# A side bank opened to VectorE's scores, history copies moved to GpSimd and the plan replaced, in a fused attention kernel with a tuned schedule

## The chip, the cores and the metric

The kernel runs on one core of a Trainium2 chip. The metric is the device time of one execution in microseconds (us); spans from the trace are about 2 us shorter than the time of the same execution. Each run also reports the mean granted clock of TensorE, 1.000 being full speed. A ratio of two kernels is the mean time of one kernel's fast runs over the mean of the other's fast runs of the same rounds, so it isn't quite the ratio of the medians that are quoted. The experiments ran on several chips, each beside runs of the kernel before; where two of them ran on different chips, the ratios are the fairer comparison.

## The reference, cut to what matters

```python
# x: 2048 tokens x 640, bf16; two branches of 32 heads of 20
A: scores = q @ k.T / sqrt(20); p = softmax(scores); o_A = (p @ v) @ woA      # all 2048 keys
B: keys at distance 0, 2, 4 .. 14 only; softmax over the 8; o_B = (...) @ woB
g = sigmoid(x . gate_w);   out = g * o_A + (1 - g) * o_B
```

Branch A is nearly all of the work: 32 groups (8 sets of four heads by 4 query blocks) of 64 units. A **unit** is 128 keys by 512 queries of one head, so there are 2048 units, and each needs an exponential of 128 x 512.

## The kernel before

A unit's exponential is made by ScalarE or by VectorE. ScalarE takes two or three units in one instruction, a **visit**. VectorE adds a constant and reads the bits as a number (`uD`), and for accuracy makes three shifted copies (`eD`) of every four such units, a **quad**; each copy costs TensorE one more round of products with the values. The program uses eight banks of PSUM, the memory that TensorE writes: two score buffers of three banks, an output bank, and a side bank for everything else (projections, branch B, the output product), called side work here.

```python
BANKS = [(sbank, 0), (score[0], 1024), (score[1], 1024)]   # side bank; third bank of each score buffer

# side work asks for a bank: the side bank wins when both are free
for b in range(NB):
    if not bank_used[b] and b != xheld[0] and (best is None or
            max(bank_free[b], now) < max(bank_free[best], now)):
        best = b
...
# next_tile: three units if the third bank of this buffer is free, else two;
# a unit for VectorE ("ride") can only have that same third bank
free = not bank_used[x] and bank_free[x] <= now + XTOL and not crowded(x)
n = 3 if free else 2
...
    if len(us) == 2 and not ride:
        ride = wanted([...])          # is VectorE early enough, is a quad open or may one be opened?
        if ride: break
```

The program orders its instructions while it is built. It keeps an assumed clock for each engine, and at each visit decides from these clocks what goes next: side work, fillers (matmuls with a zero operand or into a free bank, which keep TensorE busy), VectorE's units. Some eighteen thresholds steer it, and `PLAN` can change them at every tenth visit. The end of its assumed clocks is called the **scheduler's estimate** below. It is no measurement.

Of the kernel before, what the change touches and what calls it, by code (L numbers as in the profile page):

```python
# [9 lines left out]
I16 = mybir.dt.int16  # L10
ALU = mybir.AluOpType
# [39 lines left out]
    0: ((0.34, 0.64), 0.37, 6.3, 2.5, 0.51, -1.0, -0.1, 11.8, 4.5, 7.2, 0.52, 0.47, 4.4, 1.86, 0.0, 0.85, 2, 0.0),  # L51
    10: ((0.34, 0.64), 0.37, 6.3, 2.5, -0.17, -1.0, -0.1, 13.02, 4.5, 7.2, 0.52, 0.47, 4.4, 1.86, 0.0, 0.85, 2, 0.0),
    20: ((0.34, 0.64), 0.21, 6.3, 6.6, -0.17, -1.0, -0.1, 13.02, 4.5, 8.28, 0.52, 0.47, 4.4, 1.86, 0.0, 0.85, 2, 0.0),
    30: ((0.28, 0.52), 0.35, 2.5, 6.6, 0.49, -1.55, -0.55, 9.24, 6.7, 7.2, 0.53, 0.57, 4.23, 4.64, 0.02, 0.85, 2, 1),
    50: ((0.28, 0.52), 0.35, 2.5, 6.6, 0.49, -1.55, -0.55, 9.24, 6.7, 7.2, 0.25, 0.57, 4.23, 4.64, -0.13, 0.85, 2, 1),
    60: ((0.28, 0.52), 0.35, 2.5, 6.6, 0.49, -1.55, -0.55, 9.24, 6.7, 7.2, 0.53, 0.57, 4.23, 4.28, 0.16, 0.85, 2, 1),
    70: ((0.28, 0.52), 0.1, 2.5, 6.6, 0.49, 0.2, -0.55, 9.24, 6.7, 7.2, 0.5, 0.57, 4.23, 4.64, 0.02, 0.85, 2, 1),
    80: ((0.28, 0.52), 0.34, 2.5, 5.5, 0.49, -1.55, -0.62, 9.24, 7.0, 7.2, 0.53, 0.57, 4.55, 4.64, 0.02, 0.85, 2, 1),
    90: ((0.28, 0.52), 0.3, 2.5, 6.6, 0.49, -1.55, -0.55, 9.24, 6.7, 7.8, 0.5, 0.57, 4.23, 4.64, 0.02, 0.85, 2, 1),
    110: ((0.28, 0.52), 0.3, 2.5, 6.6, 0.49, -1.55, -0.55, 8.84, 6.7, 7.8, 0.5, 0.57, 4.23, 4.64, 0.02, 0.85, 2, 0),  # L60
    120: ((0.28, 0.52), 0.3, 5.5, 6.6, 0.49, -1.34, -0.55, 8.84, 6.7, 7.8, 0.5, 0.57, 4.23, 4.64, 0.05, 0.85, 2, 0),
    130: ((0.28, 0.52), 0.19, 5.5, 6.3, 0.49, -0.24, -0.53, 9.24, 6.7, 11.3, 0.53, 0.57, 4.23, 4.93, -0.13, 0.89, 2, -3),
    140: ((0.28, 0.52), 0.3, 2.5, 2.5, 0.87, -1.55, -0.55, 8.84, 6.7, 7.8, 0.5, 0.57, 3.8, 4.64, 0.02, 0.85, 2, 0),
    170: ((0.28, 0.52), 0.3, 2.5, 2.5, 0.87, -1.28, -0.55, 8.42, 6.7, 7.8, 0.5, 0.54, 3.8, 4.64, 0.02, 0.85, 2, 0),
    180: ((0.28, 0.52), 0.39, 6.6, 2.5, 0.87, -1.55, -0.65, 10.03, 6.7, 7.8, 0.5, 0.57, 3.8, 3.83, 0.02, 0.87, 2, -3),
    190: ((0.28, 0.52), 0.19, 2.5, 2.5, 0.7, -1.55, -0.55, 7.32, 6.7, 7.8, 0.5, 0.5, 3.8, 2.96, 0.02, 0.85, 2, -3),
    200: ((0.23, 0.54), 0.35, 2.5, 2.5, 0.87, -1.55, -0.55, 7.13, 6.7, 7.71, 0.5, 0.57, 3.46, 4.13, 0.02, 0.86, 2, -3),
    210: ((0.28, 0.52), 0.3, 2.5, 2.5, 0.9, -1.55, -0.6, 7.13, 6.7, 7.71, 0.5, 0.49, 3.46, 4.64, 0.02, 0.85, 2, -3),
    220: ((0.32, 0.54), 0.3, 2.5, 2.5, 1.16, -1.55, -0.6, 7.13, 6.7, 7.71, 0.5, 0.49, 3.46, 4.64, 0.02, 0.85, 2, -3),
    230: ((0.28, 0.52), 0.3, 2.5, 2.5, 0.9, -1.55, -0.6, 7.61, 6.7, 7.71, 0.5, 0.49, 3.46, 4.64, 0.02, 0.81, 2, -3),  # L70
    250: ((0.28, 0.52), 0.3, 2.5, 2.5, 0.9, -1.48, -0.27, 7.13, 4.5, 7.32, 0.5, 0.36, 3.46, 4.64, 0.02, 0.66, 2, -3),
    280: ((0.28, 0.52), 0.3, 2.5, 2.5, 0.9, -1.48, -0.27, 7.13, 4.5, 7.32, 0.5, 0.41, 3.46, 4.64, 0.02, 0.66, 2, -3),
    290: ((0.28, 0.52), 0.3, 2.5, 5.5, 0.9, -1.6, -0.6, 7.13, 6.7, 10.69, 0.5, 0.49, 3, 4.64, 0.02, 0.67, 2, -3),
    310: ((0.28, 0.52), 0.3, 2.5, 5.5, 0.9, -1.6, -0.6, 14.73, 6.7, 10.69, 0.5, 0.49, 5.63, 4.64, 0.02, 0.67, 2, -3),
    320: ((0.28, 0.52), 0.3, 2.5, 5.5, 1.26, -1.56, -0.6, 7.13, 6.7, 10.69, 0.5, 0.53, 3, 4.64, 0.02, 0.67, 2, -3),
    330: ((0.27, 0.53), 0.26, 2.5, 5.5, 0.58, -1.6, -0.6, 7.13, 4.5, 10.54, 0.5, 0.49, 3, 4.64, 0.11, 0.67, 2, -3),
    340: ((0.27, 0.53), 0.3, 2.5, 5.5, 0.9, -1.5, -0.6, 7.13, 7.0, 10.54, 0.41, 0.49, 3.17, 4.64, 0.2, 0.67, 2, -3),
    350: ((0.27, 0.53), 0.26, 1.0, 5.5, 0.58, -1.6, -0.6, 7.13, 4.5, 10.54, 0.5, 0.49, 3, 4.64, 0.02, 0.69, 1, -3),
    360: ((0.28, 0.52), 0.37, 2.5, 5.5, 1.26, -1.56, -0.6, 7.13, 6.7, 10.69, 0.5, 0.53, 5.91, 4.64, 0.02, 0.67, 2, -3),
    400: ((0.28, 0.52), 0.37, 2.5, 5.5, 1.26, -1.56, -0.6, 7.13, 4.5, 10.69, 0.5, 0.53, 5.91, 4.64, 0.02, 0.67, 2, -3),  # L80
    410: ((0.23, 0.54), 0.22, 2.5, 6.3, 1.26, -1.56, -0.6, 7.13, 6.7, 10.69, 0.5, 0.53, 5.35, 4.64, 0.02, 0.6, 2, -3),
    420: ((0.24, 0.49), 0.3, 2.5, 5.5, 1.26, -1.56, -0.59, 7.13, 6.7, 10.69, 0.5, 0.53, 6.0, 4.64, 0.02, 0.67, 2, -3),
    430: ((0.24, 0.49), 0.3, 2.5, 5.5, 1.26, -1.56, -0.59, 7.13, 6.7, 10.69, 0.51, 0.53, 6.0, 4.64, 0.02, 0.67, 2, -3),
    450: ((0.26, 0.56), 0.3, 2.5, 5.5, 1.26, -1.56, -0.59, 7.13, 6.7, 10.69, 0.5, 0.53, 6.0, 4.64, 0.02, 0.67, 2, 0),
    480: ((0.26, 0.56), 0.3, 2.5, 5.5, 1.26, -1.4, -0.59, 9.8, 6.7, 10.69, 0.5, 0.53, 6.0, 4.64, 0.02, 0.67, 2, 0),
    500: ((0.26, 0.56), 0.3, 2.5, 5.5, 1.26, -1.56, -0.59, 7.13, 6.7, 10.69, 0.5, 0.53, 6.0, 4.64, 0.02, 0.76, 2, -1.5),
    510: ((0.26, 0.56), 0.3, 2.5, 5.5, 1.26, -1.56, -0.09, 7.13, 6.7, 10.69, 0.5, 0.53, 6.0, 4.64, 0.02, 0.76, 2, -3),
    530: ((0.21, 0.59), 0.3, 2.5, 6.6, 1.26, -1.56, -0.43, 7.13, 6.7, 10.69, 0.5, 0.53, 6.0, 4.64, -0.23, 0.76, 2, -3),
    540: ((0.21, 0.58), 0.3, 6.6, 5.5, 1.26, -0.43, -0.09, 7.13, 6.7, 10.33, 0.5, 0.53, 6.0, 4.64, 0.08, 0.76, 2, -3),
    550: ((0.21, 0.59), 0.3, 2.5, 6.6, 1.26, -1.56, -0.43, 7.13, 6.7, 11.31, 0.49, 0.53, 6.0, 4.64, -0.36, 0.76, 2, -3),  # L90
    570: ((0.2, 0.61), 0.3, 2.5, 6.6, 1.26, -1.56, -0.43, 7.13, 6.7, 10.69, 0.5, 0.53, 6.0, 4.64, -0.23, 0.76, 2, -3),
    580: ((0.2, 0.56), 0.3, 2.5, 5.5, 1.26, -1.56, 0.15, 9.66, 6.7, 8.54, 0.49, 0.48, 6.0, 4.64, -0.36, 0.76, 2, -3),
    590: ((0.2, 0.56), 0.26, 2.5, 1.0, 1.26, -1.56, 0.15, 7.13, 6.7, 11.31, 0.49, 0.31, 6.0, 4.64, -0.36, 0.76, 2, -3),
    600: ((0.28, 0.45), 0.32, 2.5, 5.5, 1.26, -0.49, -0.43, 10.79, 5.5, 10.35, 0.57, 0.53, 6.0, 4.64, -0.33, 0.66, 2, -3),
    630: ((0.28, 0.45), 0.32, 2.5, 5.5, 0.96, -0.49, -0.43, 10.79, 5.5, 10.35, 0.65, 0.53, 6.0, 4.64, -0.33, 0.66, 2, -3),
    660: ((0.28, 0.45), 0.32, 2.5, 5.5, 0.96, -0.1, -0.27, 10.79, 5.5, 10.35, 0.65, 0.53, 6.0, 4.64, -0.33, 0.66, 2, -3),
    670: ((0.28, 0.5), 0.32, 2.5, 5.5, 1.11, -0.49, -0.43, 10.79, 6.2, 10.35, 0.65, 0.55, 6.5, 4.81, -0.39, 0.62, 2, -3),
    690: ((0.3, 0.64), 0.32, 2.5, 2.5, 0.49, -1.0, -0.1, 11.8, 5.5, 7.2, 0.52, 0.47, 4.4, 4.0, 0.0, 0.85, 2, 0.0),
    700: ((0.42, 0.48), 0.32, 6.3, 5.5, 0.76, -0.49, -0.43, 10.79, 5.5, 10.35, 0.65, 0.53, 6.0, 4.64, -0.33, 0.63, 2, -3),
# [220 lines left out]
def _build(ctx, nc, A_x, A_wqkv, A_wo, B_wqkv, B_wo, gate_w, out):  # L320
# [208 lines left out]
    xheld = [None]  # L529
# [295 lines left out]
    def gen_bproj(u):  # L825
# [7 lines left out]
        for grp in (((0, 0), (0, 1)), ((0, 2), (0, 3)), ((1, 0), (1, 1)), ((1, 2), (1, 3)), ((0, 4), (1, 4)),  # L833
# [4 lines left out]
            if u > 0 and m > 0 and f0 == 0:  # L838
                bb, key = ((kB, "kB"), (vB, "vB"))[m - 1]
                TB(0.15, lambda e, bb=bb: e.tensor_copy(bb[:, :, 0:PADB], bb[:, :, TOK:TOK + PADB]), reads=[key], writes=[key], port=True)  # L840
# [300 lines left out]
    def step(ent, limit, force):  # L1141
# [14 lines left out]
        elif req[0] == "bank":  # L1156
            best = None
            for b in range(NB):
                if not bank_used[b] and b != xheld[0] and (best is None or max(bank_free[b], now) < max(bank_free[best], now)):
                    best = b  # L1160
            if best is None or sum(bank_used) == NB - 1 or (not force and bank_free[best] > now):
                return False
            if best and not force and (ent[0] > xprio() or any(o_[3][0] == "pe" and o_[3][2] <= now + 0.3 for o_ in gens)):
                return False
            bank_used[best] = True
            bank_own[best] = ent
            send = best
# [9 lines left out]
    BOFF = 0.0  # L1177
    BOOST = 4.4
# [192 lines left out]
    rides = []  # L1371
    UNIT = 0.46
# [9 lines left out]
    BALL = 172.0  # L1382
# [80 lines left out]
    def next_tile():  # L1463
# [6 lines left out]
        ride = None  # L1470
        while len(us) < n and cur["g"] < NG:
# [11 lines left out]
            if len(us) == 2 and not ride:  # L1483
                ride = wanted([j for j in range(4) if all(uu % 4 != j for uu in us)])
                if ride:
                    break
# [291 lines left out]
```

## Time and profile before

| | before |
|---|---|
| time, median of 3 | 836.07 us |
| busy: TensorE / VectorE / ScalarE / GpSimd | 789.3 / 683.7 / 803.9 / 138.7 us of a span of 835.4 |
| units on ScalarE / VectorE | 1724 / 324 |
| visits: with three units for ScalarE / with two / with one | 255 / 479 / 1 |

Read such a table with the counts beside the busy times: a busy engine may be busy with padding (TensorE has fillers), and an engine with many small waits may still be the one that sets the pace. The lines behind the table are in the prediction. The columns are: length; busy time (and instructions) of TensorE, weight loads, VectorE, ScalarE, GpSimd; then the granted clock, the DMA share and GB/s.

```profile
440.00:450.00 10.00, 8.06 (x152) 3.11 (x152) 7.72 (x17) 10.00 (x11) 1.10 (x1) 1.00 0.12 39
450.00:460.00 10.00, 8.41 (x116) 3.09 (x116) 7.20 (x13) 8.78 (x8) 2.29 (x3) 0.83 0.16 41
```

The clock of the second stretch is 0.83: apart from the last half microsecond, the trace holds one dip to half speed, 3.4 us long, from 456.2 us on. ScalarE lost 1.2 us in that stretch, almost 0.5 us of it in a gap at 452 us, before the dip.

### The profile page before, as it was taken

Reading aid. Unit: us, or ns where it says so; the run is one execution under the profiler, and the core shown is the slowest. Engines: PE = TensorE matmul, PEld = TensorE weight load, DVE = VectorE, ACT = ScalarE, POOL = GpSimd, SP = SyncE. Lnnn points to the kernel's source line nnn. Section 1 sums busy time; section 2 is a strip of 40 time slices with the busy share of each in tenths; the row PEclk is TensorE's granted clock in tenths of the full one; section 3 lists DMA queues with packets and bytes.
Section 4 is the critical chain, followed back from the end, with each engine's and each line's share of the span. In section 5 each row is a group of like instructions: output and inputs, shape, how many; then the busy total and the mean of one; then the engine's idle time right before and its main releaser. Section 6 shows DMA issues by size and latency. Waiting matters only on the chain.

```text
span 835.4 us, 29602 instructions
## 1 busy us (share of the span) xinstructions
PE 789.3 (94%) x12599; PEld 289.9 (35%) x12601; DVE 683.7 (82%) x1205; ACT 803.9 (96%) x767; POOL 138.7 (17%) x180
## 2 busy tenths in 40 slices
PE   8999999999999899989998999999999999998997
PEld 4333323334333332333233333333333333333223
DVE  7567888889888887978797988798898898887873
ACT  4999999999999999999999999999999999999994
POOL 5013013431111111011111011111102111101110
PEclk9999999999999999999999999999999999999999
DMA  9112112200111110011001011110011001101100
GB/s 313 30 37 44 33 25 45 73 13 19 29 37 29 29 30 20 7 42 32 20 18 41 18 20 29 36 42 9 5 39 30 10 20 25 38 6 31 32 6 34
DMA packets 45016, 29.15 MB, mean 35 GB/s; under 512 B 27204, under 2 KB 43684, under 8 KB 44884
## 3 DMA queue, kind: packets, MB, share of 16 engines
q1 hardware_dynamic: 44596, 26.92, 12.4%
q8 instruction: 100, 1.64, 0.8%
q10 hardware_dynamic: 288, 0.33, 0.1%
q14 instruction: 32, 0.26, 0.1%
HBM read 11.94 MB, written 2.62 MB: 17 GB/s over the span
## 4 chain that ended last, share of the span: by engine, by line
PE 54%; ACT 30%; issue 10%; DVE 5%; DVEq 0%; ACTq 0%
ACT ebuf L1538 30%; PE score L1515 17%; PE obank L1583 13%; PE side L557 13%; PE score L557 5%; PE obank L1604 2%; DVE uD L1528 1%; PE side L1604 1%; DVE eD L797 1%; PE obank L459 1%; PE score L1230 1%; PE side L885 1%; DVE stage L869 0%; PE score L1604 0%; DVE stage L970 0%
## 5 line engine op out<-in xcount | busy, mean ns | idle before, releaser
L1538 ACT ACTIVATE ebuf<-score 128x1024 bf16<-128x1024 f32 (+1 forms) x735 | 792.6, 1237 | 11.6 <-PE score L1515 9.7
L1515 PE MATMUL score<-qT,kT 32*128 32x512 bf16 x2048 | 291.9, 384 | 31.6 <-ACT ebuf L1538 20.6
L1528 DVE TENSOR_SCALAR uD<-score 128x512 int16<-128x512 f32 x324 | 217.2, 683 | 38.4 <-PE score L1515 36.1
L797 DVE TENSOR_SCALAR eD<-uD 128x2048 int16<-128x2048 int16 x243 | 168.1, 722 | 7.9 <-PE obank L1583 7.2
L1515 PEld LDWEIGHTS score<-qT,kT 32*128 32x128 bf16 x2048 | 75.1, 91 | 282.7 <-ACT ebuf L1538 137.6
L1583 PE MATMUL obank<-ebuf,vA 128*21 128x512 bf16 x1724 | 161.3, 385 | 2.2 <-ACT ebuf L1538 1.8
L789 POOL TENSOR_TENSOR vS<-vA,vw 128x252 bf16<-128x252 bf16 x81 | 61.0, 757 | 291.5 <-PE obank L1583 256.3
L557 PE MATMUL side<-xT,kvw 128*32 128x256 bf16 (+1 forms) x2530 | 103.0, 281 | 3.1 <-DVE qkvB L853 1.4
L1583 PE MATMUL obank<-eD,vS 128*21 128x512 bf16 x972 | 84.1, 382 | 0.0
L557 PEld LDWEIGHTS side<-xT,kvw 128*32 128x32 bf16 x2530 | 59.3, 96 | 37.9 <-issue 22.0
L764 POOL TENSOR_TENSOR rcp<-rcp,gA 128x16 f32<-128x16 f32 x31 | 11.3, 365 | 351.9 <-DVE rcp L762 351.9
L1583 PEld LDWEIGHTS obank<-ebuf,vA 128*21 128x21 bf16 x1724 | 38.6, 89 | 82.3 <-issue 69.5
L970 DVE TENSOR_TENSOR stage<-qkvB,repB 128x1280 bf16<-128x1280 bf16 x64 | 52.9, 856 | 0.7 <-DMA repB<-eB 0.7
L869 DVE TENSOR_TENSOR stage<-qkvB 128x1280 bf16<-128x1280 bf16 x64 | 51.4, 830 | 0.1
L853 DVE CAST qkvB<-side 128x512 bf16<-128x512 f32 (+1 forms) x72 | 41.9, 591 | 10.5 <-PE side L557 10.5
L557 PE MATMUL side<-stage,ident 128*32 128x512 bf16 (+1 forms) x736 | 47.4, 345 | 1.2 <-DVE uD L744 0.5
L1604 PE MATMUL obank<-xT,zero 128*32 128x512 bf16 x444 | 37.9, 385 | 0.0
L770 POOL TENSOR_TENSOR oN<-oTt,rcp 128x512 bf16<-128x512 f32 x31 | 33.0, 1065 | 2.4
L1583 PE MATMUL obank<-uD,vA 128*21 128x512 bf16 x324 | 31.7, 382 | 0.0
L758 DVE STREAM_TRANSPOSE oTt<-obank 128x512 f32<-128x512 f32 x32 | 22.7, 709 | 9.0 <-PE obank L1583 8.9
L1583 PEld LDWEIGHTS obank<-eD,vS 128*21 128x21 bf16 x972 | 24.0, 92 | 17.4 <-issue 4.1
L557 PE MATMUL side<-woA_d,oTd 128*32 128x128 bf16 (+1 forms) x580 | 28.8, 293 | 0.0
(173 smaller groups left out, 555.5 us busy)
## 6 DMA issues: line engine op xcount, KB each, us to landing
repB<-eB SPq DMA_DIRECT2D x128, 32.0 KB
WqP<-in_A_wqkv_dram SPq DMA_DIRECT2D x16, 160.0 KB
stage<-in_B_wqkv_dram SPq DMA_DIRECT2D x1, 2400.0 KB
oTd<-oN SPq DMA_DIRECT2D x108, 20.0 KB
qT<-dst SPq DMA_DIRECT2D x104, 20.0 KB
out_dram<-outsb SPq DMA_DIRECT2D x12, 160.0 KB
kvw<-in_A_wqkv_dram SPq DMA_DIRECT2D x2, 800.0 KB
oTd<-in_A_x_dram SPq DMA_DIRECT2D x2, 640.0 KB
```

The costliest lines, as they stand in the source:

```text
L557: ins = e.matmul(o[j:k, :], l(j) if callable(l) else l[:, j:k], r, start=(first and i == 0), stop=(last and i == n - 1), skip_group_check= ...
L770: T(en, c2, lambda e: e.tensor_tensor(oo, ii, ib, ALU.mult), reads=["rcp", "oTt"], writes=["oN0"])
L789: T("pool", 0.7, lambda e: e.tensor_tensor(vS[:, d % 2, :, :], _ap(vA, (kb * NQ + q) * 4 * DV, [[0, K - 1], [1, 4 * DV]]), _ap(vw, 0, [[1, ...
L797: T("dve", 0.11 + 0.1334 * n, lambda e, k=k, sl=sl: e.tensor_scalar(eD[:, sl % NS, 0:512 * n].bitcast(I16), uD[d % 2][:, 0:512 * n].bitcas ...
L853: t = TB(dvc(n * TOK), lambda e, o=o, i=i: e.tensor_copy(o, i), reads=[("side", b)], writes=[key])
L869: TB(dvc(CN * TOK, 2), lambda e, w=w, ks=ks: e.tensor_tensor(prodB(w), qB[:, :, :], ks, ALU.mult), reads=["qB", "kB"], writes=[("prod", w) ...
L970: TB(dvc(CN * TOK, 2), lambda e, w=w, vs=vs, rr=rr: e.tensor_tensor(prodB(w), vs, rr, ALU.mult), reads=["vB", ("repB", w4 % NR)], writes=[ ...
L1515: ins = e.matmul(o, kT[32 * j:32 * j + 32, q, kb * P:(kb + 1) * P], qT[g % NQT][32 * j:32 * j + 32, :], start=True, stop=True)
L1528: t = T("dve", 0.69, lambda e: e.tensor_scalar(uD[d % 2][:, 512 * i:512 * (i + 1)].bitcast(I16), side[x], UOFF, 0.0, op0=ALU.add, op1=ALU. ...
L1538: exps[s] = T("act", actc(512 * n), lambda e: e.activation(ebuf[s % NE][:, 0:512 * n], score[s % 2][:, 0:512 * n], ACTF.Exp, scale=LN2 / S ...
L1583: ins = e.matmul(obank[32 * j:32 * j + DV, :], v, src, start=(kb == 0), stop=(last and k >= len(lst) - 4), skip_group_check=True)
L1604: ins = e.matmul(o[32 * j:32 * j + 32, :], w[:, 32 * j:32 * j + 32] if best else w[:, :], xT[:, 0, 0:512], start=bool(best), stop=bool(bes ...
```

## The change

The intent: let VectorE's unit go to the side bank when that is spare, so that a visit can hold three units for ScalarE and one for VectorE, and so that a visit of two can still give VectorE a unit while side work holds its third bank. The 14 copies that carry branch B's last columns of keys and values over to the next block go to GpSimd. All of `PLAN` is new, with one more threshold (`SBP`, from which priority on side work waiting for a bank keeps VectorE out).

```diff
-    0: ((0.34, 0.64), 0.37, 6.3, 2.5, 0.51, -1.0, ... 0.85, 2, 0.0),
+    0: ((0.32, 0.63), 0.32, 2.5, 2.5, 0.49, -1.0, ... 0.85, 2, 5.5, 0.0),
  (all rows of PLAN are replaced; the last row's visit was 700 and is now 720)
-                TB(0.15, lambda e, bb=bb: e.tensor_copy(bb[:, :, 0:PADB], ...), ..., port=True)
+                T("pool", 0.3, lambda e, bb=bb: e.tensor_copy(bb[:, :, 0:PADB], ...), ...)
+        def spare():
+            return not bank_used[0] and bank_free[0] <= now + XTOL and not any(
+                ent[3][0] == "bank" and ent[0] <= SBP for ent in gens)
             if len(us) == 2 and not ride:
-                ride = wanted([...])
-                if ride:
-                    break
+                if spare():
+                    ride = wanted([...]); rb = 0          # side bank; a third unit still follows
+                else:
+                    ride = wanted([...]); rb = x          # third score bank, as before
+                    if ride:
+                        break
+        if len(us) == 2 and not ride and not free and spare():
+            ride = wanted([...]); rb = 0
-            if not bank_used[b] and b != xheld[0] and ...
+            if not bank_used[b] and b not in xheld[0] and ...
-BALL = 172.0
+BALL = 170.0
```

## The prediction

> **What bounds the kernel now.** I began with the busy shares, went on to the slices, then the groups, the same groups with shapes kept apart, the waits, and last the stretches of 100 us. Shares and slices first:
>
> ```profile
> PE 789.3 (94%) x12599; PEld 289.9 (35%) x12601; DVE 683.7 (82%) x1205; ACT 803.9 (96%) x767; POOL 138.7 (17%) x180
> ...
> PE   8999999999999899989998999999999999998997
> ...
> DVE  7567888889888887978797988798898898887873
> ACT  4999999999999999999999999999999999999994
> ```
>
> ScalarE is full in every slice but the first and the last. TensorE looks nearly as full, so I asked the groups what each is full of:
>
> ```profile
> L1538 ACT ACTIVATE ebuf<-score 128x1024 bf16<-128x1024 f32 (+1 forms) x735 | 792.6, 1237 | 11.6 <-PE score L1515 9.7
> ...
> L1528 DVE TENSOR_SCALAR uD<-score 128x512 int16<-128x512 f32 x324 | 217.2, 683 | 38.4 <-PE score L1515 36.1
> L797 DVE TENSOR_SCALAR eD<-uD 128x2048 int16<-128x2048 int16 x243 | 168.1, 722 | 7.9 <-PE obank L1583 7.2
> ...
> L1604 PE MATMUL obank<-xT,zero 128*32 128x512 bf16 x444 | 37.9, 385 | 0.0
> ```
>
> A unit of scores is 128 keys by 512 queries; there are 2048. One exponential of ScalarE (a visit) takes two or three units; VectorE takes 324 by an integer trick, and three shifted copies of every four. ScalarE waited only 11.6 us in 735 visits. The last line is filler matmuls with zeros: TensorE is padded, to keep its clock. All fillers, read by stretch from 30 us on, come to 60.2 us of TensorE's busy time, so TensorE has room that its 94% hides. Shapes kept apart:
>
> ```profile
> L1538 ACT ACTIVATE ebuf<-score 128x1024 bf16<-128x1024 f32 x479 | 463.4, 1082 | 6.4 <-PE score L1515 5.0
> L1538 ACT ACTIVATE ebuf<-score 128x1536 bf16<-128x1536 f32 x255 | 359.2, 1530 | 5.1 <-PE score L1515 4.4 <-ACT ebuf L1538 0.2
> ```
>
> The two busy times overlap each other and are not to be added. From the counts: 479 x 2 + 255 x 3 + one of a single unit = 1724, and 1724 + 324 = 2048. In the old code a visit with a VectorE unit is never one of three, since that unit sits in the third bank of the score buffer. So 255 visits are 3 + 0, about 324 are 2 + 1, and about 156 are 2 + 0.
>
> The waits of TensorE and VectorE show how the three lock:
>
> ```profile
> PEld score L1515 <- ACT ebuf L1538: 137.6, 339, 1.2
> ...
> DVE uD L1528 <- PE score L1515: 36.1, 79, 1.6
> ...
> PEld score L1515 <- DVE uD L1528: 24.4, 53, 0.9
> ...
> ACT ebuf L1538 <- PE score L1515: 9.7, 24, 2.1
> ```
>
> TensorE waits for ScalarE to free score buffers far more than ScalarE waits for scores. The chain of waits names TensorE for 54% of the span because the ordering runs through it, but a chain among engines with such small gaps isn't proof that TensorE bounds. I take ScalarE's amount of work as the bound, and VectorE's capacity as what limits moving more of it away.
>
> ```profile
> 100.00:200.00 100.00, 98.36 (x1453) 33.78 (x1449) 84.35 (x141) 98.83 (x97) 27.88 (x28) 1.00 0.18 41
> ...
> 600.00:700.00 100.00, 94.05 (x1455) 33.19 (x1453) 88.87 (x157) 99.18 (x102) 15.49 (x20) 1.00 0.10 23
> 700.00:800.00 100.00, 93.39 (x1549) 33.66 (x1541) 81.64 (x138) 98.87 (x89) 14.81 (x20) 1.00 0.10 26
> ```
>
> The columns are length, then the busy time of TensorE, weight loads, VectorE, ScalarE and GpSimd, then the granted clock. The clock is full. VectorE ranges from 81.64 to 88.87.
>
> **What the Trainium skill says.** "ScalarE: Activation LUTs", under "What ACT_TABLE_LOAD costs", gives 186 ns + 0.833 ns per element for an activation with immediate operands, and an overlap of about 93 ns between neighbours. That is 427 ns per unit and 93 ns per visit. The records of this trace agree on the first and are lower on the second: between exponentials with no gap the median start-to-start is 904 ns after two units and 1330 ns after three, so 426 ns per unit, and 904 - 852 = 52 ns per visit (66 from the mean end-to-end times, 919 and 1345). I use **0.426 us a unit and 0.06 us a visit**. "PSUM - Partial Sum Buffer", under "PSUM bank collisions raise a hardware error", says that two engines must not be in one bank and quadrant at once, and its specifications count eight banks. The kernel has all eight: two score buffers of three, one output, one side. A fourth unit in a visit must therefore take the side bank from the projections; no trace line shows a collision. "GPSIMD Engine Reference", under "Key points", has GpSimd share SBUF interfaces with VectorE's two-port modes and VectorE about twice as fast at elementwise work; no line here has the history copy on both engines.
>
> **The change, part by part.** (1) *Three units plus one.* Widening by itself saves almost nothing: one visit less is 0.06 us. The new plan's last stage starts at visit 720, so I take it that at least 721 of the 735 visits remain: at most 14 x 0.06 = 0.8 us. (2) *More units to VectorE.* This is where time can come from. A visit whose third bank holds a projection can now still give VectorE a unit in the side bank, and the 156 visits of 2 + 0 are the stock to draw on. A quad of four units costs VectorE 4 x 0.670 + 3 x 0.691 = 4.76 us (217.2/324 and 168.1/243), and takes 4 x 0.426 = 1.70 us off ScalarE. How many quads? From 100 to 800 us VectorE is busy 596.8 of 700 us (the sum of the seven stretches), 85.3%. If the freer choice of bank brings all of them to the best stretch's 88.87%, that is 25.3 us more. (3) *History columns.* The 14 copies show as
>
> ```profile
> L840 DVE COPY qkvB<-qkvB 128x80 bf16<-128x80 bf16 x14 | 2.4, 173 | 0.1
> ```
>
> which gives VectorE 2.4 us back: half a quad, 0.9 us of ScalarE. On GpSimd they should cost a few us in all of an engine busy 17%, beside other work. Together (25.3 + 2.4)/4.76 = 5.8, so **six quads, 24 units**: VectorE goes from 324 to 348 units, ScalarE from 1724 to 1700, and saves 24 x 0.426 = 10.2 us. (4) *TensorE pays* three extra rounds of four matmuls a quad; four side by side take about 0.22 us (starts in the timeline), so 6 x 3 x 0.22 = 4 us, which fits in the 60.2 us of fillers. (5) The plan is tuned afresh at every stage; head and tail (about 20 us before the first exponential, 12 after the last) are untouched. **Sum:** 836.1 - 10.2 - 0.6 (ten visits) = 825.3, say **825 us**, 1.3% faster.
>
> **Rivals.** *Only an exchange of banks.* Eight banks stay eight. If VectorE's score holds the side bank, a projection goes to the third score bank or waits, and the next visit is narrower. For it: several hundred projection matmuls write score banks already, and new and old visit counts look alike. Against it: the 2 + 0 visits. Alone it leaves the history copies and a little tuning: 832 to 836. *VectorE becomes the bound.* [...]its evictions come late, score banks stay shut, and TensorE then ScalarE wait; the 24.4 us of TensorE waiting for uD are its seed. With more quads than it can carry, ScalarE's idle time would grow by what its work shrank: 828 to 838. *A larger shift.* If VectorE does reach 92% from 100 to 800 us, that is 47 + 2.4 us, ten quads, 40 units, 17 us and a little for visits: 818. For it: VectorE's 36.1 us of waiting for scores is time that a better ordering could fill; against it: the side projections also need VectorE just then. *GpSimd's copy late.* Evictions of keys and values must come after it; if it queues behind a 1.07 us product there, a bank is held that long. Even 14 x 1 us would be mostly beside other work: under 3 us.
>
> **Range and chances.** The middle is six quads; between no quad (exchange, 834) and ten (818) lies most of my belief. Below 819.3 us, the 2% mark, ten quads or fewer idle gaps beside eight are needed: one in four. Slower by 2% would need the tuned plan to fail outright, which TensorE's spare fillers make unlikely. Range 814 to 833; faster 0.25, same 0.72, slower 0.03.
>
> **What would show it.** Right: exponentials still over 720 visits, more of them of 1536 columns; some 348 uD evictions and 261 eD copies; VectorE's busy time near 710 us with a share of about 86%; ScalarE still about 96% with less busy time (near 793); fillers fewer; the history copy on GpSimd under 0.5 us each. Wrong: uD still near 324 (exchange); ScalarE's idle time up by over 5 us with TensorE waiting for uD (VectorE bound); well under 720 visits, or over 364 uD evictions (larger shift).

## The result, and the profile after

The changed kernel took 833.11 us (832.65 to 833.89, 4 runs) against 836.15 us (835.97 to 837.18, 4 runs) of the kernel before; the ratio is 0.9962, with an interval of 0.9945 to 0.9979. It is 3 us faster. The prediction said 825, so its gain of 11 us was over three times too large, and the time lies just outside its range of 814 to 833. The chances (0.72 for "within 2%") were sound.

The busy shares and slices of the changed kernel:

```profile
PE 786.0 (95%) x12650; PEld 288.5 (35%) x12650; DVE 681.9 (82%) x1197; ACT 802.2 (96%) x758; POOL 133.6 (16%) x195
...
DVE  7658887689788888978897898788988878988983
ACT  4999999999999999999999999999999999999995
```

VectorE is no busier than before: the prediction looked for about 710 us. The groups, in the same columns as in the prediction:

```profile
L1563 ACT ACTIVATE ebuf<-score 128x1024 bf16<-128x1024 f32 (+1 forms) x726 | 790.7, 1232 | 9.8 <-PE score L1540 7.9
...
L1553 DVE TENSOR_SCALAR uD<-score 128x512 int16<-128x512 f32 x311 | 210.2, 685 | 53.7 <-PE score L1540 51.0
L802 DVE TENSOR_SCALAR eD<-uD 128x2048 int16<-128x2048 int16 (+1 forms) x246 | 170.9, 721 | 2.6 <-PE obank L1608 1.8
...
L1629 PE MATMUL obank<-xT,zero 128*32 128x512 bf16 x424 | 34.8, 382 | 0.0
```

With shapes kept apart, ScalarE's exponentials and VectorE's evictions from the side bank:

```profile
L1563 ACT ACTIVATE ebuf<-score 128x1024 bf16<-128x1024 f32 x455 | 442.7, 1071 | 5.8 <-PE score L1540 4.0 <-ACT ebuf L1563 0.6
L1563 ACT ACTIVATE ebuf<-score 128x1536 bf16<-128x1536 f32 x270 | 380.7, 1507 | 4.1 <-PE score L1540 3.8
```

```profile
L1553 DVE TENSOR_SCALAR uD<-side 128x512 int16<-128x512 f32 x16 | 11.0, 686 | 4.8 <-PE side L1540 4.6
```

The filler line fell, but all fillers together did not (60.6 us before, 61.8 after). The new path was used **16 times**. VectorE has 311 + 16 = 327 units, three more than before; ScalarE has 455 x 2 + 270 x 3 + 1 = 1721 in 726 visits. The history copies are on GpSimd:

```profile
L845 POOL COPY qkvB<-qkvB 128x80 bf16<-128x80 bf16 x14 | 3.9, 281 | 44.3 <-DVE stage L975 44.3
```

And the waits:

```profile
PEld score L1540 <- ACT ebuf L1563: 142.8, 346, 1.2
...
DVE uD L1553 <- PE score L1540: 51.0, 87, 2.4
...
PEld score L1540 <- DVE uD L1553: 20.5, 43, 0.9
...
ACT ebuf L1563 <- PE score L1540: 7.9, 20, 2.1
```

**Where the time came from.** The spans of the profiled runs are 835.4 and 831.5, a difference of 3.9 us. ScalarE's busy time fell from 803.9 to 802.2, by 1.7; three units at 0.426 us and nine visits at 0.06 us give 1.8. ScalarE's idle time (span less busy time) fell from 31.5 to 29.3, by 2.2. Of that, 1.0 us is two gaps, one within the dip of the kernel before and one right after it (0.64 us at 457.8 and 0.37 at 459.9), read from the trace's records; the changed kernel's trace has no dip within its span.

So part of the difference goes with the clock. The runs of the kernel before show it: of all that ran beside the experiments below, those whose clock was 1.000 had spans of 833.8 to 833.9 us, those at 0.998 had 834.1 to 836.8, those at 0.995 had 835.7 to 837.0, and one each at 0.994 and 0.993 had 838.4 and 838.0. The changed kernel's three runs at 1.000 had 830.9 to 831.5. By these few runs, which are not of the same rounds, the change is worth 2.3 to 3.0 us at full clock. (e4 below, the changed kernel's order with one engine exchanged, spread from 830.7 to 832.3 at 1.000, so these ends are not sharp.)

### The profile page after: what moved, and what is told of

Same layout as the page of the kernel before. It is cut to its first block, busy times and chain, and to the rows that moved or that the text cites. A ratio compares the mean times of both kernels' runs of the same rounds, so it can differ in the third digit from the quotient of the medians.

```text
span 831.5 us, 29660 instructions
## 1 busy us (share of the span) xinstructions
PE 786.0 (95%) x12650; PEld 288.5 (35%) x12650; DVE 681.9 (82%) x1197; ACT 802.2 (96%) x758; POOL 133.6 (16%) x195
## 4 chain that ended last, share of the span: by engine, by line
ACT 44%; PE 40%; issue 13%; DVE 3%; DVEq 0%; ACTq 0%
ACT ebuf L1563 44%; PE score L1540 12%; PE obank L1608 10%; PE side L562 9%; PE score L562 4%; PE obank L1629 1%; DVE eD L802 1%; PE score L1236 1%; PE obank L464 1%; ACT eB L919 1%; PE score L1629 0%; PE side L1629 0%; PE side L1259 0%; DVE uD L1553 0%; ACT tB L953 0%
## 5 line engine op out<-in xcount | busy, mean ns | idle before, releaser
L1540 PE MATMUL score<-qT,kT 32*128 32x512 bf16 x2032 | 289.3, 384 | 33.1 <-ACT ebuf L1563 27.2
L1553 DVE TENSOR_SCALAR uD<-score 128x512 int16<-128x512 f32 x311 | 210.2, 685 | 53.7 <-PE score L1540 51.0
L802 DVE TENSOR_SCALAR eD<-uD 128x2048 int16<-128x2048 int16 (+1 forms) x246 | 170.9, 721 | 2.6 <-PE obank L1608 1.8
L562 PE MATMUL side<-xT,kvw 128*32 128x256 bf16 (+1 forms) x2440 | 100.4, 280 | 1.7 <-DVE rQ L956 0.7
L794 POOL TENSOR_TENSOR vS<-vA,vw 128x252 bf16<-128x252 bf16 x82 | 56.5, 692 | 270.3 <-PE obank L1608 229.6
L1608 PE MATMUL obank<-eD,vS 128*21 128x512 bf16 x981 | 86.6, 379 | 0.0
L975 DVE TENSOR_TENSOR stage<-qkvB,repB 128x1280 bf16<-128x1280 bf16 x64 | 50.7, 829 | 0.2 <-DMA repB<-eB 0.2
L562 PE MATMUL side<-stage,ident 128*32 128x512 bf16 (+1 forms) x608 | 38.8, 348 | 0.1
L1629 PE MATMUL obank<-xT,zero 128*32 128x512 bf16 x424 | 34.8, 382 | 0.0
L562 PE MATMUL side<-woBp,oB 128*32 128x128 bf16 (+1 forms) x580 | 28.7, 293 | 0.7 <-DVE outsb L1113 0.5
```

The source lines that it names most:

```text
L562: ins = e.matmul(o[j:k, :], l(j) if callable(l) else l[:, j:k], r, start=(first and i == 0), stop=(last and i == n - 1), skip_group_check= ...
L794: T("pool", 0.7, lambda e: e.tensor_tensor(vS[:, d % 2, :, :], _ap(vA, (kb * NQ + q) * 4 * DV, [[0, K - 1], [1, 4 * DV]]), _ap(vw, 0, [[1, ...
L802: T("dve", 0.11 + 0.1334 * n, lambda e, k=k, sl=sl: e.tensor_scalar(eD[:, sl % NS, 0:512 * n].bitcast(I16), uD[d % 2][:, 0:512 * n].bitcas ...
L975: TB(dvc(CN * TOK, 2), lambda e, w=w, vs=vs, rr=rr: e.tensor_tensor(prodB(w), vs, rr, ALU.mult), reads=["vB", ("repB", w4 % NR)], writes=[ ...
L1540: ins = e.matmul(o, kT[32 * j:32 * j + 32, q, kb * P:(kb + 1) * P], qT[g % NQT][32 * j:32 * j + 32, :], start=True, stop=True)
L1553: t = T("dve", 0.69, lambda e: e.tensor_scalar(uD[d % 2][:, 512 * i:512 * (i + 1)].bitcast(I16), side[rb], UOFF, 0.0, op0=ALU.add, op1=ALU ...
```

## The experiments

Theories. **A**: the kernel is bound by ScalarE's work, VectorE's capacity limits what can be moved, and each part of the change is worth the time it carries (the prediction). **B**: the plan fits one exact sequence of decisions, and the parts open almost no new places. **C**: TensorE is close to being a second bound, so that VectorE's capacity alone isn't what limits its share.

### One part undone, plan left as it is: e1, e2, e3

```diff
# e1, in the changed kernel
-            return not bank_used[0] and bank_free[0] <= now + XTOL and not any(
+            return False and not bank_used[0] and bank_free[0] <= now + XTOL and not any(
# e2, in the changed kernel (e3: the opposite edit in the kernel before)
-                T("pool", 0.3, lambda e, bb=bb: e.tensor_copy(...), reads=[key], writes=[key])
+                TB(0.15, lambda e, bb=bb: e.tensor_copy(...), reads=[key], writes=[key], port=True)
```

Expected of e1:

> The changed kernel with its new plan, but VectorE never given the side bank (the test for a spare side bank always says no). The side bank was used only 16 times in 327. Theory A (the part is worth what it carries): 16 units at most go back to ScalarE, 16 x 0.426 = 6.8 us, so 833 to 841 us. Theory B (the new plan fits one exact sequence of decisions, and any change of a decision throws the rest off): far more is lost, as the scheduler's own estimate says: 866 us against 834, with 280 units on VectorE in place of 327, so 860 to 870 us; ScalarE's busy time then rises by 47 x 0.43 = 20 us.

Expected of e2:

> The changed kernel with its new plan, but the 14 history copies back on VectorE, told to the scheduler too. The copies take 2.4 us of VectorE in all. Theory A: half a quad, 833 to 836 us. Theory B (fit of the plan): the scheduler's own estimate is 856 us with 308 units on VectorE, so 850 to 860 us.

Expected of e3:

> The kernel before with its old plan, the only edit being the 14 history copies on GpSimd. Theory A: it frees 2.4 us of VectorE, so 834 to 837 us. Theory B (fit of the plan): the scheduler's own estimate is 859 us, with 746 visits and still 324 units on VectorE, so 853 to 864 us.

Measured: e1 867.77 us (ratio to the kernel before 1.0371; 280 units on VectorE, ScalarE busy 824.6 us, 22 more), e2 857.72 (1.0251), e3 858.23 (1.0257). All three cost 20 us or more, as theory B expected. e3 even loses 21 us although it *relieves* VectorE by 2.4 us, with VectorE's units unchanged at 324. Its exponentials:

```profile
L1538 ACT ACTIVATE ebuf<-score 128x1024 bf16<-128x1024 f32 (+1 forms) x746 | 794.3, 1204 | 19.9 <-PE score L1515 17.7 <-ACT ebuf L1538 0.3
```

Eleven more visits, and ScalarE idle for 8 us more before them. The larger half of the loss comes after them. The last exponential ended 9.7 us later than in the kernel before (833.5 us against 823.8), but the program went on for 24.8 us after it, in place of 11.6: side work was left over, with 14.9 us of its matmuls after the last exponential in place of 6.1. ScalarE's longest wait there, in the kernel before and in e3:

```profile
ACT stage L1082 <- PE score L1063: 6.9, 1, 6.9
```

```profile
ACT stage L1082 <- PE side L1063: 19.0, 1, 19.0
```

Running the program's scheduler again, off the chip, shows where the courses part: e3 gives each visit the same units as the kernel before up to visit 223, and others from there (e2 follows the changed kernel up to visit 196, e1 up to 19). Every later row of the plan then meets a state that it was not tuned for. **Undoing one part of a change in such a kernel doesn't measure the part.** It has to be undone with the order frozen, or with a plan searched anew.

### The order frozen, the copies on VectorE again: e4

```diff
+        t.real = real or stream
-        self.lists[stream].append(t)
+        self.lists[t.real].append(t)          # and dependencies are keyed by t.real
-                T("pool", 0.3, lambda ..., reads=[key], writes=[key])
+                T("pool", 0.3, lambda ..., reads=[key], writes=[key], real="dve")
```

> The changed kernel with every instruction in its place, except that the 14 history copies are handed to VectorE at the same place in the order; the scheduler still thinks that they run on GpSimd, so no decision changes. Both theories that put the gain elsewhere expect the same time as the changed kernel within 0.3% (831 to 836 us); if moving the copies were itself the gain of 3 us, it would go back to 836 us or more. VectorE's busy time should rise by about 2.4 us.

Measured: 832.63 us (832.50 to 834.14, ratio 0.995), VectorE busy 683.9 us against 681.9. The time is that of the changed kernel. With this order, which engine makes the copies is worth nothing. (On average a copy took 173 ns on VectorE, in the kernel before, and 281 ns on GpSimd, in the changed one.)

### The order frozen, one engine's work cut: e5, e6, e7

```diff
# e5 (wrong result on purpose)
+        w = 512 * n if n > widest[s % NE] else 480 * n
-            ebuf[s % NE][:, 0:512 * n], score[s % 2][:, 0:512 * n], ACTF.Exp, scale=LN2 / STEP),
+            ebuf[s % NE][:, 0:w], score[s % 2][:, 0:w], ACTF.Exp, scale=LN2 / STEP),
# e6 (wrong result on purpose)
+            c = 512 * n if n > filled[sl % NS] else 256 * n
-                eD[:, sl % NS, 0:512 * n].bitcast(I16), uD[d % 2][:, 0:512 * n].bitcast(I16), ...
+                eD[:, sl % NS, 0:c].bitcast(I16), uD[d % 2][:, 0:c].bitcast(I16), ...
# e7
-  ins = e.matmul(o[32 * j:32 * j + 32, :], ..., xT[:, 0, 0:512], ...)       # filler
+  ins = e.matmul(o[32 * j:32 * j + 32, 0:64], ..., xT[:, 0, 0:64], ...)
```

Expected of e5:

> The changed kernel, every instruction in its place, but each exponential covers 480 columns a unit in place of 512 after the first ones in each buffer (wrong result on purpose; the rest of the buffer holds old values). It takes about 1721 x 32 x 0.833 ns = 46 us off ScalarE, 5.7%. If ScalarE's amount of work is what bounds: down by 35 to 46 us, to 787 to 798 us. If TensorE bounds it just as much (rival): down by under 15 us, with ScalarE's idle time up by over 30 us.

Expected of e6:

> The changed kernel, every instruction in its place, but each shifted copy on VectorE covers half its columns after the first ones (wrong result on purpose). It takes some 243 x 0.25 = 60 us off VectorE. If VectorE bounds the kernel directly: down by over 20 us. If VectorE only limits how many units it can be given, which a frozen order cannot change: down by under 8 us, to 825 to 834 us, and VectorE's idle time rises by what its work fell.

Expected of e7:

> The changed kernel, every instruction in its place, but each filler matmul on TensorE has 64 columns in place of 512 (result stays right). It takes some 40 us of the 61 us of filler time off TensorE. If TensorE has room, as its fillers suggest: 830 to 836 us, same, unless the granted clock drops. If TensorE bounds: down by over 10 us.

The chain of waits of the changed kernel, for comparison:

```profile
ACT 44%; PE 40%; issue 13%; DVE 3%; DVEq 0%; ACTq 0%
```

Measured: **e5** 818.77 us, 14 us less than the changed kernel (16 by the ratios, 0.977 against 0.9962). From its page the busy line, the chain of waits, and its exponentials:

```profile
PE 783.0 (96%) x12648; PEld 288.2 (35%) x12650; DVE 679.4 (83%) x1197; ACT 770.8 (94%) x758; POOL 134.9 (17%) x195
...
PE 64%; ACT 18%; DVE 8%; issue 5%; SPq 3%; DMA 1%; DVEq 0%; ACTq 0%
...
L1567 ACT ACTIVATE ebuf<-score 128x960 bf16<-128x960 f32 (+2 forms) x726 | 758.6, 1130 | 25.7 <-PE score L1540 16.6 <-ACT ebuf L1567 0.6 <-PE side L1540 0.5
```

ScalarE's busy time fell by 31.4 us, less than the 46 expected, and only 14 of those came off the time. The rest turned into ScalarE waiting: its wait before exponentials rose from 9.8 to 25.7 us, mostly for TensorE's scores. The time met the rival's number (down by under 15 us) by the medians and just missed it by the ratios; ScalarE's idle time rose by 16 us (from 29.3 to 45.3) and not by over 30, while less was cut than expected. The chain turned from ScalarE to TensorE; alone that would be weak, as the kernel before, 3 us from the changed one, has TensorE at 54%. With the idle time it says that in this order TensorE is close behind ScalarE.

**e6** 834.19 us: 58.8 us off VectorE (681.9 to 623.1), and no gain. VectorE does not bound directly.

**e7** 844.15 us, **11 us slower** (9 by the ratios), though all that was done was to shorten TensorE's padding. The fillers' busy time fell from 61.8 to 25.9 us, near the expected 40, but TensorE's by only 13, because its other matmuls took longer: the score matmuls of the first line below had 289.3 us and 384 ns in the changed kernel. That line, and two stretches:

```profile
L1540 PE MATMUL score<-qT,kT 32*128 32x512 bf16 x2032 | 294.6, 391 | 52.0 <-ACT ebuf L1563 44.4
```

```profile
100.00:200.00 100.00, 95.26 (x1389) 32.98 (x1381) 79.50 (x140) 97.64 (x94) 27.40 (x29) 0.95 0.17 39
200.00:300.00 100.00, 87.61 (x1492) 34.61 (x1489) 83.47 (x144) 98.19 (x90) 12.84 (x21) 0.95 0.11 26
```

The granted clock fell to 0.95 in these stretches (1.00 in the changed kernel) and to 0.978 over the whole run; the trace holds six dips to half speed within its span, of 3.4 to 10.2 us each. The fillers are not room that can be had for the asking: in this run, less of them meant less clock. This was the escape clause of the expectation, and it decided.

### Plans searched anew with equal effort: e8, e9, e13, e14

For each of four codes (old, new, side bank alone, copies alone) the plan was thrown away and searched again from one default row, with the same number of trials, by the scheduler's estimate. (e13 also has `BALL`, the assumed pace of branch B, back at 172.) No such plan is as good as the two that came with the kernels, but all had the same search.

Expected of e8 and e9:

> The code of the kernel before with a plan searched anew from one default row, two passes of some 60 trials at each tenth visit, judged by the scheduler's own estimate alone (849.1 us; 304 units on VectorE). It is the yardstick of the next run, not a candidate. 845 to 853 us on the chip, as the estimate has been within 0.5% so far.

> The code of the changed kernel with a plan searched in the same way and with the same number of trials (estimate 847.6 us; 307 units on VectorE, 15 by the side bank). If the two parts of the change have the worth that was predicted, 24 more units on VectorE, this should be 8 to 11 us below the run of the old code with a fresh plan. If they open almost no places, it should be within 4 us of it, with under 5 more units on VectorE.

Expected of e13 and e14:

> The changed code with the history copies back on VectorE, so that only the freedom of the side bank is left, with a fresh plan of the same search (estimate 850.6 us, 307 units on VectorE, 16 by the side bank). If this part carries the gain: near the new code's fresh plan, 846 to 848 us. If the difference between the two fresh plans is the luck of the search: anywhere from 847 to 853 us.

> The changed code with the side bank shut to VectorE, so that only the copies on GpSimd are left, with a fresh plan of the same search (estimate 851.0 us, 308 units on VectorE). If the copies carry the gain: 846 to 848 us. If neither part does: near the old code's fresh plan, 849 to 853 us.

| code, fresh plan | estimate | measured (fast runs) | clock of these | units on VectorE | by the side bank |
|---|---|---|---|---|---|
| old (e8) | 849.1 | 851.28 (851.07 to 851.89) | 1.000 | 304 | 0 |
| new (e9) | 847.6 | 846.85 (846.80 to 847.39) | 0.995 to 0.998 | 307 | 15 |
| side bank alone (e13) | 850.6 | 847.94, 848.89, 850.90 | 0.997 to 1.000 | 307 | 16 |
| copies alone (e14) | 851.0 | 858.66 (857.83 to 859.43) | 0.994 to 0.998 | 308 | 0 |

New is 4.4 us below old, with three more units on VectorE, close to what the tuned pair showed (3 us, three units); the time falls between the two expectations of e9 (8 to 11 us, or within 4), the units meet the second. Side bank alone lies between the two in time. It ran on another chip; by the ratios to the kernel before it equals new (1.0138 and 1.0132; old 1.0184). Copies alone is the slowest (1.0247), outside both ranges that were expected of it, and 7.7 us above its own estimate with a lower clock. That fits "the side bank carries the gain and the copies carry none", but it doesn't prove it: one search stands behind each row, so how far luck alone moves such a plan isn't known. What e14 lost against its estimate isn't explained either. What the table does show is the number of units: it hardly depends on the code.

One of e13's four runs, the profiled one, took 1339.2 us and is left out of the table as slow. Its stretches:

```profile
600.00:690.00 90.00, 86.06 (x1398) 29.92 (x1394) 74.22 (x129) 88.29 (x84) 10.25 (x15) 1.00 0.10 26
700.00:1330.00 630.00, 629.65 (x2218) 115.52 (x2214) 110.79 (x182) 147.06 (x120) 15.46 (x24) 0.16 0.01 4
```

From 699 us to the end TensorE was granted 0.16 of its clock. No other run here did that, and nothing here tells why.

### What holds the number of VectorE's units: e10, e11, e15

```diff
# e10: the edit of e6, and the scheduler is told
-            T("dve", 0.11 + 0.1334 * n, ...
+            T("dve", 0.11 + 0.0667 * n, ...
# e11: half of the matmuls that sum branch B's taps
-                   for w in (0, 4, 1, 5, 2, 6, 3, 7)]
+                   for w in (0, 4, 1, 5)]
# e15: side work takes a score bank where it may, the side bank only otherwise
-   if not bank_used[b] and ... max(bank_free[b], now) < max(bank_free[best], now)): best = b
+   if not bank_used[b] and ... max(bank_free[b], now) <= max(bank_free[best], now)): best = b
    (and where the rules forbid the score bank, it falls back to the side bank)
```

All three have fresh plans by the same search, one search each, so they are to be compared with e9 (846.85 us, 307 units) and with the reserve just stated.

Expected of e10:

> The changed code with shifted copies of half the columns (wrong result on purpose), this time told to the scheduler, and a plan searched anew as for the other fresh plans (estimate 840.7 us; 319 units on VectorE). It frees some 55 us of VectorE. If VectorE's capacity is what held the number of its units, as the prediction took it, 55/4.8 = 11 quads, 44 more units and some 20 us less than the fresh plan of the changed code. If something else holds it as well: 12 more units and 5 to 9 us less.

Expected of e11:

> The changed code with half of the matmuls that add up B's eight taps left out (wrong result on purpose), some 20 us off TensorE and nothing off VectorE or ScalarE, told to the scheduler, plan searched anew (estimate 841.8 us; 328 units on VectorE). If only VectorE's capacity held the number of its units: no more than 310 of them, same time as the fresh plan of the changed code within 3 us. If TensorE's room holds it too: about 20 more units on VectorE and 4 to 8 us less, although VectorE got no relief.

Expected of e15:

> The changed code with one rule turned round: a projection takes a score bank where it may, and the side bank only otherwise, so that the side bank is left to VectorE more often; fresh plan of the same search (estimate 849.1 us, 312 units on VectorE, 23 by the side bank, 737 visits). If places in the side bank are what VectorE lacks: many more than 23 units there and 5 us or more below the new code's fresh plan. If it is an exchange of banks: narrower visits (249 of three units against 292), and 846 to 852 us, no gain.

Measured: **e10** 841.38 us with 298 + 21 = 319 units. VectorE had a busy time of 617.4 us against e9's 665.4, so most of the relief was left unused. Capacity alone would have given 44 units and 20 us; it gave 12 and 5.5, the second expectation.

**e11** 841.44 us with 328 units (wrong result). Its evictions, and VectorE's total:

```profile
PE 807.1 (96%) x13069; PEld 298.7 (36%) x13069; DVE 683.0 (81%) x1198; ACT 802.6 (96%) x748; POOL 138.6 (17%) x195
...
L1511 DVE TENSOR_SCALAR uD<-score 128x512 int16<-128x512 f32 x307 | 205.7, 683 | 39.1 <-PE score L1498 36.4 <-PE side L874 0.8
```

A smaller relief of TensorE brought more units than the relief of VectorE did: 21 more, with VectorE 18 us busier and ScalarE 8 us less busy (802.6 against 810.2). So VectorE in e9 had capacity that it didn't use. That TensorE's room was what it lacked is the likely reading, not a shown one. TensorE's own busy time didn't fall, as the search put in more fillers (123 us of them, against 80 in e9). And the edit has a second effect: by the scheduler's clocks, branch B's sums hold a bank for 166 us in all in place of 214, so places came free as well. No run separates the two.

**e15** 853.1 us, 6 us slower than e9, with 312 units, 23 of them by the side bank, and visits of three down from 304 to 264 in the traces. This looks like an exchange of banks: what the side bank gives to VectorE, the third score bank takes from ScalarE. (By the ratios it is 4 us slower. Its estimate was 849.1, so some of that may be the estimate's error; a gain it is not.) But the rule turned less than it seems: by the scheduler's own count the side bank still went to side work 145 times of 223, against 160 in e9. e15 tests a small shift of places, and doesn't tell what many free ones would give.

The scheduler's own record of its decisions in the changed kernel says why the side bank was used so seldom; it comes from running the scheduler in `kernel.py` off the chip. For its 141 visits of two units with nothing for VectorE:

```
third score bank held by side work in 72, released but not yet drained in 37,
kept back for waiting side work in 32; and the side bank at that moment
  held by side work                     88
  released, but not yet drained         40
  spare, but side work waits for it      9
  spare                                  4   (VectorE late, or no quad could be opened)
```

In 61 of the 141 a quad was open and VectorE early enough, so a spare bank would have been used there; in the other 80 VectorE was too late (38) or no quad could be opened (42). And for its 257 visits of three units with nothing for VectorE: VectorE too far behind in 124, both quad buffers still in use in 65, two quads already in flight in 52, other causes in 16. A spare bank would have changed none of these.

### A try at beating both: e12

The new plan's later stages, from visit 300 on, were searched further.

> The changed code with its own plan, whose later stages were searched further by the scheduler's estimate (833.1 us against 834.3 for the plan as it came; 327 units on VectorE either way, 725 visits, 20 units by the side bank). A try at beating both kernels: 831 to 834 us, probably not to be told from the changed kernel's 833.1.

Measured: 834.21 us (832.19 to 837.69, 6 runs; ratio 0.9959 beside 836.93 for the kernel before in the same rounds). It can't be told from the changed kernel. The expectation held.

## Why the prediction was wrong, point by point

**The step that failed** is (2), "More units to VectorE": "A visit whose third bank holds a projection can now still give VectorE a unit in the side bank, and the 156 visits of 2 + 0 are the stock to draw on", from which came six quads. VectorE got 3 more units in place of 24. The stock was not there. Side work takes the side bank first and goes to a score bank when the side bank is in use, which the code quoted above says; so a busy third bank nearly always means a busy side bank. Of the 141 such visits, 137 had it held, not drained, or wanted. The rule could be read before the prediction, and the stock looked at: the same count on the kernel before finds 155 such visits (the prediction's 156 less the visit of one unit), with the side bank held in 106, not drained in 38, spare but with side work waiting in 5, and spare in 6. e15 turned the rule round in part: a few more places in the side bank, fewer visits of three, no gain.

**The limit behind it** was also wrong in part. The step took VectorE's capacity as what limits moving work, and the best stretch's 88.87% as within reach everywhere. From 100 to 800 us the changed kernel's VectorE was busy 597.5 us (the sum of its seven stretches), against 596.8. In e10 some 55 us less work on VectorE brought 12 units and not 44, so something else holds their number as well; e11 points to TensorE's room or to the time that side work holds banks, and leaves open which.

**"TensorE has room that its 94% hides"** was wrong, and the sentence before it had said why: the padding is there to keep the clock. e7 took work out of the fillers and lost 9 to 11 us with the clock at 0.978; e5 took 31 us off ScalarE and got 14 to 16.

**ScalarE's amount of work as the bound** was half right: the sum of units and visits reproduces its busy time (1.8 worked out, 1.7 measured), but in a frozen order only about half of a cut in it came through (e5).

**Visits.** "At most 14" fewer visits, under 0.8 us: right, nine fewer. The start-to-start times after two and three units were 905 and 1331 ns, as before.

**History copies.** Their cost on GpSimd was right (0.28 us each, beside other work). The half quad that they were to give VectorE was not shown: e4, with the order frozen, can only say that the copies themselves cost no time, and four units more in e14 than in e8 lie within what one search each can tell.

**The rivals.** "Only an exchange of banks ... 832 to 836" met the time, and its sign, uD evictions near 324, was seen. Its mechanism was not: it has the next visit narrower, and the changed kernel has more visits of three (270 against 255). The side bank was simply spare too seldom for much to be exchanged. The rival of VectorE as the bound was not seen: ScalarE's idle time fell, and TensorE's waits for uD went from 24.4 to 20.5 us. The 92% that the prediction lets VectorE reach for its larger shift was reached in no run (83% at most, in e5). The exchange was named, and its evidence (projection matmuls already in score banks) was weighed too low against a stock that had only been counted, not looked at.

**What the prediction's sum did not have** is the clock. It read 1.00 in three stretches and called the clock full, but the trace has a dip of 3.4 us, and the two gaps of ScalarE in and after it are 1.0 us, about a quarter of the difference between the two profiled spans.

What stays open: how much of the 2.3 to 3.0 us at full clock is the side bank's 16 uses and how much is that the new plan happens to be a better one. The equal searches (e8 against e9) agree with the former, but with one search for each code they can't exclude the latter. That the result stayed within 2%, as forecast, is partly luck: the prediction reached it by way of 24 units, and three moved.

## What to carry to other kernels

Before counting opportunities for a resource, check whether the thing that creates each opportunity also takes the resource away: here a busy third bank implied a busy side bank, by the order in which banks are handed out. In a kernel whose order is tuned decision by decision, undo a part with the order frozen or with an equal search for each side, since a plain undo measures the tuning (21 to 35 us here, where all parts together were worth 3). And padding on TensorE may be what holds its clock, as in e7, so it isn't free room.

## What the Trainium skill lacked or had wrong

- "ScalarE: Activation LUTs", under "What ACT_TABLE_LOAD costs": 186 ns + 0.833 ns per element less about 93 ns of overlap leaves 93 ns for each visit. Back to back, the traces show 904 ns (two units) and 1330 ns (three) from start to start, which is 426 ns a unit as stated but 52 ns a visit; from end to end (917 and 1343 ns) it is 65 ns. A single exponential after an idle ScalarE took 1023 and 1450 ns, 16 ns less than stated (1039 and 1466); the averages of 1082 and 1530 ns in the profile lines hold the overlap with a neighbour and are not to be set beside it.
- "TensorE: Matmul & The Clock Gate", Part 1: its dips to half clock in windows of about 3.4 us agree with the traces (3.4, 6.8 and 10.2 us long in e7). It puts them down to idle stretches and, in a later section of Part 1, to short idling between groups of matmuls, and gives no busy share at which they stop: e7 with 92% had six, the kernel before with 94% had one at 456 us, and which run has one differs: the kernel before spread over spans from 833.8 us at a clock of 1.000 to 838.4 at 0.994.
- The same page lists half, full and 13/16 clock, and a case of one quarter for over 50 us. It has no state like that of e13: 0.16 of the clock for the last 638 us of one execution on a single core.
- "GPSIMD Engine Reference", under "Key points", calls VectorE about twice as fast at elementwise work. For a copy of 128 x 80 bf16, which has one input, the traces show 173 ns on VectorE and a median of 249 ns on GpSimd, 1.4 times as long; but single ones took up to 713 ns in the changed kernel and 847 ns in e14, which raised the means to 281 and 429 ns. The one of 713 ns ran beside a shifted copy of VectorE that took 1087 ns where the median is 685. The same section names contention between the two engines' SBUF interfaces for some of VectorE's instructions, without a duration; that it is the cause here isn't shown.
